# Steps of r, k, w and v laid in planes from the third tile on, and u times r on ScalarE

## The chip, the cores and the metric

The kernel runs on one core of a Trainium2 chip. Its engines are TensorE (matmuls, PE in the profile, with its weight loads as PEld), VectorE (DVE), ScalarE (ACT), GpSimd (POOL) and SyncE (SP, which issues the DMAs). The metric is the device time of one execution in microseconds. On-chip memory (SBUF) has 128 partitions; matmul results land in PSUM banks.

## The reference

Two parts follow each other. The first is a recurrence over 768 steps, for 4 batches and 8 heads of 48 channels:

```
state = 0
for t in range(S):
    cur = einsum('bhd,bhe->bhde', u[None] * k[t], v[t])
    y[t] = einsum('bhd,bhde->bhe', r[t], state + cur)
    state = w[t][:, :, :, None] * state + einsum('bhd,bhe->bhde', k[t], v[t])
```

The second takes y as 3072 rows of 384 numbers and computes `gelu(y @ w_in) @ w_out`, with w_in 384 x 2048 and w_out 2048 x 384. All is float32.

## The kernel before

The 3072 rows are eight tiles of 384 steps, numbered x = 0 to 7; two tiles make one batch. For each tile there is an attention() generator (the recurrence) and an mlp() generator (the two matrix products). PLAN, a string for each tile, says step by step which generator is advanced next: mlp of tile x-1, attention of tile x, the front part of attention of tile x+1 ("f"), the loads ("l") and sums. So the order on every engine is written out beforehand, and each engine works through its own list in that order.

In attention(), partitions hold channels (two heads of 64 rows, 48 of them used) and the free dimension holds steps. Steps are cut in chunks of C = 64. Inside a chunk the recurrence is a triangular 64 x 64 matrix for each head, built in `a_sb` (named `at` in the code, with source steps on partitions and target steps in columns). Tiles 0 and 1 build it by halving (`halves`). From tile 2 on it is built in this way:

- Blocks of FINE = 4 steps: for each distance 0 to 3, the products of r and k (L404 for distance 0, with u; `apart`, L398, for the others) are summed over channels by `transposed_sums` (L391) and placed by small matmuls (L595). `kx` holds the products, one stretch of it for each step inside a block: the writes of L404 and L398 jump from stretch to stretch with every element.
- Blocks of 16 and 64 steps (`quarters`, h = 4 and h = 16): `plain` (L573, ScalarE) and `lay_out` (L578 and L579, VectorE) put scaled copies of r in `kx`; matmuls (L604) multiply them by k; the results are copied to `a_sb` under masks (L637) at h = 4 and by rows (L620) at h = 16. L658, L665 and L669 scale r and k for the next level by running products of w (`tot`, L424).
- The blocks of 4 are copied under `fine_mask` (L687), two copies of 768 columns.

Then VectorE transposes k (L552) and DMAs move its blocks; kv_ps (L749) gives each chunk's share of the state, L764 chains the states; `inside` (L790) multiplies `a_sb` by v into y_ps; `fences` (L802) read one element of each y bank; L832 adds the product of r and the states to the same banks; ScalarE copies y to `xT` (L858, L855), from which the mlp reads (L1011, L1237).

In `halves` tiles ScalarE scales r by u (L414). In tiles 2 to 7 the steps of r, k and w lie in order: r4, k4 and w4 view them as "p (m a) -> p m a" with a = 4, so that `r4[:, :, 3:4]` is every fourth word. L432 (`times`) multiplies such slices in place.

A load of a tile takes r first, then w, then k, in three DMAs each, then v; w and k have one buffer, r has two. A float32 matmul in the program stands as two records in the trace.

Of the kernel before, what the change touches and what calls it, by code (L numbers as in the profile page):

```python
# [21 lines left out]
C = 64  # L22
G = 64
# [41 lines left out]
def kernel(  # L65
# [87 lines left out]
    places = bufs[0][:, 3 * ALL - FINE * 128:].rearrange("p (a r) -> p a r", a=FINE)  # L153

    def load_first():

        t = bufs[0]
        loaded[0] = [None, None]
        size = 3 * NP * T // units_of(0)
        order = [(i, 2) for i in range(units_of(0))] + [(i, part) for i in range(units_of(0)) for part in (0, 1)]  # L160
        for n, (i, part) in enumerate(order):
            s = slice(i * size + part * size // 3, i * size + (part + 1) * size // 3)
            nc.sync.dma_start(out=t[:, s], in_=rkw[0, :, s])
            if n == 0:
                nc.sync.dma_start(out=u_sb, in_=u)
# [113 lines left out]
    nc.gpsimd.iota(t_all, pattern=[[1, C]], base=0, channel_multiplier=0)  # L279
    nc.gpsimd.iota(t_block, pattern=[[1, C // FINE], [0, FINE]], base=0, channel_multiplier=0)  # L280
    for i, h in enumerate(QUARTERS[:1]):
# [10 lines left out]
    def make_fine():  # L292
        nc.vector.tensor_tensor(out=fine_mask, in0=s_qs[FINE], in1=t_block, op=ALU.is_equal)
        nc.vector.tensor_tensor(out=later, in0=t_all, in1=s_qs[1], op=ALU.is_ge)
        nc.vector.tensor_tensor(out=fine_mask, in0=fine_mask, in1=later, op=ALU.bitwise_and)

        nc.gpsimd.memset(places, 0.0)
        for z in range(4):
            o = slice(z * 32, (z + 1) * 32)
            v = places[o]  # L300
            v = bass.AP(tensor=v.tensor, offset=v.offset, ap=[v.ap[0], [128 + 1, FINE], [FINE, 32]])
            nc.gpsimd.tensor_copy(out=v, in_=ident[o, o].unsqueeze(1).to_broadcast([32, FINE, 32]))

    def make_quarter_masks():
        make_fine()
        yield
        for (h, a), m_q in m_qs.items():
            nc.vector.tensor_tensor(out=quarter[h][a], in0=s_qs[h][:, 0:m_q.shape[1]], in1=m_q, op=ALU.is_equal)
            yield
# [56 lines left out]
    def attention(x, unit):  # L366
# [19 lines left out]

        r4, k4, w4 = (z.rearrange("p (m a) -> p m a", a=FINE) for z in (r, k, w))
        n_m = n_u // FINE

        def transposed_sums(o, e, n):  # L390
# [4 lines left out]
        def apart(e, n):  # L395

            o = sum(FINE - i for i in range(1, e)) * n_m
            nc.vector.tensor_mul(kx[:, o:o + n * n_m].rearrange("p (a m) -> p m a", a=n), k4[:, :, 0:n], r4[:, :, e:e + n])  # L398
            return o

        if x >= 2:
            for q in range(qs):
                m_q = slice(q * T // FINE, (q + 1) * T // FINE)
                nc.vector.scalar_tensor_tensor(out=kx[:, 0:n_u].rearrange("p (a m) -> p m a", a=FINE)[:, m_q],  # L404
                                               in0=r4[:, m_q], scalar=u_sb[:, q:q + 1], in1=k4[:, m_q],
                                               op0=ALU.mult, op1=ALU.mult)
            yield
            transposed_sums(0, 0, FINE)
            yield
        else:  # L410

            rus = [kx[:, b * Q * T:(b + 1) * Q * T] for b in parts]
            for q in range(qs):
                nc.scalar.activation(out=rus[q // Q][:, q % Q * T:(q % Q + 1) * T], in_=r[:, q * T:(q + 1) * T], func=AF.Copy,  # L414
                                     scale=u_sb[:, q0 + q:q0 + q + 1])
            rucs = [ru.rearrange("p (i c t) -> p i c t", c=2, t=C) for ru in rus]
# [3 lines left out]
        for h in LEVELS:  # L420
            nb = n_u // (2 * h)
            t2 = tot[h].rearrange("p (n two) -> p n two", two=2)
            tot[2 * h] = tot_sb[:, at_tot:at_tot + nb]
            nc.vector.tensor_mul(tot[2 * h], t2[:, :, 0], t2[:, :, 1])  # L424
            at_tot += nb
            if x >= 2 and h == 2:
                yield
        if x >= 2:
# [18 lines left out]

            w_01 = tot[2].rearrange("p (m two) -> p m two", two=2)[:, :, 0:1]
            times(k4[:, :, 0:3], w4[:, :, 3:4].to_broadcast([128, n_m, 3]))
            yield  # L450
            times(r4[:, :, 3:4], w4[:, :, 2:3])
            times(r4[:, :, 1:2], w4[:, :, 0:1])
            times(r4[:, :, 2:4], w_01.to_broadcast([128, n_m, 2]))
            yield
# [101 lines left out]
        def quarters():  # L556
# [5 lines left out]

            def views(h):
                m = C // 4 // h
                r4 = r.rearrange("p (n m four j) -> p n m four j", m=m, four=4, j=h)
                t4 = tot[h].rearrange("p (n m four) -> p n m four", m=m, four=4)
                ends = (0, 3 * C // 4, 5 * C // 4, 6 * C // 4)
                return m, r4, t4, *(rx[:, :, i:j].rearrange("p n (m x) -> p n m x", m=m) for i, j in zip(ends, ends[1:]))

            def plain(h):  # L570
                m, r4, t4, s0, s1, s2 = views(h)
                for z, f in ((s0[:, :, :, 0:h], 1), (s1[:, :, :, 0:h], 2), (s2, 3)):
                    nc.scalar.copy(out=z, in_=r4[:, :, :, f, :])  # L573

            def lay_out(h):
                m, r4, t4, s0, s1, s2 = views(h)
                z = s1[:, :, :, h:]
                nc.vector.tensor_mul(z, r4[:, :, :, 3, :], t4[:, :, :, 2:3].to_broadcast(z.shape))  # L578
                nc.vector.tensor_mul(s0[:, :, :, h:], s1, t4[:, :, :, 1:2].to_broadcast(s1.shape))  # L579

# [4 lines left out]
            for h in QUARTERS:  # L585
# [36 lines left out]
                def copy_quarters(first, behind, d):  # L622
# [5 lines left out]
                    if m == 1:  # L628
                        copy_rows(first, behind, d, slice(None))
                        return  # L630
                    an = at[:, :, first:behind].rearrange("p g n (m x) -> p g n m x", m=m)
                    o = 0
                    for a in range(3):
                        w_q = (3 - a) * C // 4
                        mask = quarter[h][a].rearrange("p (m x) -> p m x", m=m).unsqueeze(1).unsqueeze(1)
                        data = d[:, :, :, o:o + w_q].rearrange("p g n (m x) -> p g n m x", m=m)
                        nc.vector.copy_predicated(out=an[:, :, :, :, (a + 1) * h:], mask=mask.to_broadcast(data.shape), data=data)  # L637
                        o += w_q
# [17 lines left out]

                z = r4[:, :, :, 1:, :].rearrange("p n m b j -> p n m (b j)")
                nc.vector.tensor_mul(z, s0, t4[:, :, :, 0:1].to_broadcast(z.shape))  # L658
                yield
                if not last:  # L660
                    plain(4 * h)
                k4 = k.rearrange("p (n four j) -> p n four j", four=4, j=h)
                z = k4[:, :, 0:2, :].rearrange("p n b j -> p n (b j)")
                t2 = tot[2 * h].rearrange("p (n two) -> p n two", two=2)
                nc.vector.tensor_mul(z, z, t2[:, :, 1:2].to_broadcast(z.shape))  # L665
                yield
                z = k4.rearrange("p n (b two) j -> p n b two j", two=2)[:, :, :, 0, :]
                tz = t4.rearrange("p n m (b two) -> p (n m) b two", two=2)[:, :, :, 1:2]
                nc.vector.tensor_mul(z, z, tz.to_broadcast(z.shape))  # L669
                yield  # L670
# [11 lines left out]
                if h == FINE:  # L682
                    mask = fine_mask.rearrange("p (m b) -> p m b", b=FINE).unsqueeze(1)
                    for g in range(2):
                        data = fine_of(ds[-1], g).rearrange("p (b n) -> p n b", n=n_b)
                        data = data.unsqueeze(2).to_broadcast([128, n_b, C // FINE, FINE])
                        nc.vector.copy_predicated(out=at[:, g].rearrange("p n (m b) -> p n m b", b=FINE),  # L687
                                                  mask=mask.to_broadcast(data.shape), data=data)
                        yield

# [88 lines left out]
        def inside():  # L779

            for b in range(np_):
# [5 lines left out]
                for i in range(NI):  # L787
                    for p in range(2):
                        for g in range(2):
                            nc.tensor.matmul(y[p][half[g ^ swap(b)], i * C:(i + 1) * C], lhsT=vs(b, i, g)[half[p]],  # L790
                                             rhs=at[half[p], g, b * NI + i, :], start=(i == 0), stop=True, skip_group_check=True)
                ys.append((y, None if split else y_ps))
# [19 lines left out]
        else:  # L812
# [4 lines left out]
            yield  # L817
            inside()
            fences()
            yield  # L820

        for i in range(NI):
            for p in range(2):
                for b in range(np_):
                    q, c3 = divmod(i, N3)
                    for g in range(2):
                        c = 2 * c3 + (p + g) % 2
                        src, c0 = (st, c - 1) if c else (before, NC - 1)
                        if src is None:
                            continue  # L830
                        o = ((parts[b] * Q + q) * NC + c0) * D
                        nc.tensor.matmul(ys[b][0][c % 2][half[g ^ swap(b)], i * C:(i + 1) * C],  # L832
                                         lhsT=src[half[g], o:o + G], rhs=rc[half[g], b, i, c % 2],
                                         start=False, stop=True, skip_group_check=True)
# [642 lines left out]
```

## Time and profile before

| | |
|---|---|
| median of 3 runs | 589.5 us (588.08 to 589.55) |
| profiled execution | 592.28 us, span 590.5 us |
| busy in the span | PE 571.7, DVE 462.9, ACT 275.9, POOL 8.0 us |
| granted TensorE clock | 1.0 |
| L790, a_sb by v | 768 records, 96 a tile |
| L832, r by the states | 704 records, 80 or 96 a tile |

A row of a group reads: line, engine, operation, output and inputs, shapes, count, then total busy us and mean ns of one, then the idle time of the engine before them and what ended it. In the list of waits a row gives who waited, for whom, the total in us, how many times, and the longest. In the row of tenths each digit is the busy share of one fortieth of the span. Matmuls are pipelined: their recorded lengths (218 ns for 64 columns) overlap, so the price of one is taken from the length of a whole group in the chain divided by its records.

### The profile page before, as it was taken

How to read it: one execution, taken by the hardware profiler on the slowest of the kernel's cores; microseconds unless marked ns; L12 is line 12 of the kernel's file. 1: busy time of each engine (PE TensorE's matmuls, PEld its weight loads, DVE VectorE, ACT ScalarE, POOL GpSimd, SP SyncE). 2: the span in 40 equal slices, each digit the busy share in tenths (PEclk: the TensorE clock that was granted, in tenths of full speed). 3: DMA queues.
4: the chain of work that ended last, by engine and by line, in shares of the span. 5: the costliest groups of instructions: out<-in, count | busy, mean ns of one | idle time of the engine just before them, and what ended most of it. 6: DMA issues, size and time to landing. Idle time of an engine off the chain costs nothing. (4 is left out here: it accounts for less than half of the span.)

```text
span 590.5 us, 17425 instructions
## 1 busy us (share of the span) xinstructions
PE 571.7 (97%) x7505; PEld 508.1 (86%) x7517; DVE 462.9 (78%) x907; ACT 275.9 (47%) x640; POOL 8.0 (1%) x21
## 2 busy tenths in 40 slices
PE   7769999999999999999999999999999999999998
PEld 3566666766799999999999999999998999999997
DVE  7879767988968986787859987688758998975532
ACT  2458889323612558046461468145560465523400
POOL 3100000000000000000000000000000000000000
PEclk9999999999999999999999999999999999999999
DMA  7649661120142301341023311330015200210000
GB/s 245 206 138 354 211 232 56 34 88 2 29 139 78 109 3 31 98 125 38 1 42 104 122 38 21 93 115 7 3 31 163 73 2 2 41 39 8 1 14 33
DMA packets 51004, 46.80 MB, mean 79 GB/s; under 512 B 31728, under 2 KB 36080, under 8 KB 50928
## 3 DMA queue, kind: packets, MB, share of 16 engines
q1 hardware_dynamic: 50832, 45.62, 25.4%
q8 instruction: 59, 0.97, 0.7%
q14 instruction: 17, 0.14, 0.1%
q10 hardware_dynamic: 96, 0.07, 0.1%
HBM read 36.24 MB, written 4.72 MB: 69 GB/s over the span
## 5 line engine op out<-in xcount | busy, mean ns | idle before, releaser
L1011 PE MATMUL h_ps<-xT,w_in_sb 128*128 128x192 f32 x408 | 81.2, 330 | 0.7 <-DVE o_sb L1360 0.6
L1011 PEld LDWEIGHTS h_ps<-xT,w_in_sb 128*128 128x128 f32 x408 | 67.8, 190 | 3.7 <-ACT g L1043 1.2
L1223 PE MATMUL h_ps<-xT,w_in_sb 128*128 128x384 f32 x192 | 64.1, 490 | 0.1
L1223 PEld LDWEIGHTS h_ps<-xT,w_in_sb 128*128 128x128 f32 x192 | 35.9, 190 | 23.9
L1237 PE MATMUL o_ps<-w_out_sb,g 128*128 128x192 f32 x224 | 39.5, 326 | 0.0
L1237 PEld LDWEIGHTS o_ps<-w_out_sb,g 128*128 128x128 f32 x224 | 36.9, 190 | 0.3
L620 ACT COPY a_sb<-d 32x256 f32<-32x256 f32 (+8 forms) x90 | 32.6, 362 | 4.6 <-PE d L604 3.1
L1237 PE MATMUL o_ps<-w_out_sb,f 128*128 128x192 f32 x176 | 31.7, 330 | 0.0
L1237 PE MATMUL o_ps<-t,g 128*128 128x192 f32 x176 | 31.4, 329 | 0.0
L1237 PE MATMUL o_ps<-w_out_sb,e 128*128 128x192 f32 x176 | 31.3, 328 | 0.0
L1237 PE MATMUL o_ps<-t,s 128*128 128x192 f32 x176 | 30.9, 327 | 0.0
L1237 PE MATMUL o_ps<-t,e 128*128 128x192 f32 x176 | 30.9, 327 | 0.0
L637 DVE COPY_PREDICATED a_sb<-quarter,d 128x480 f32<-128x480 uint8 (+5 forms) x54 | 23.1, 437 | 8.6 <-PE d L604 7.3
L465 PEld LDWEIGHTS d<-rkw 64*64 64x64 f32 x1152 | 19.1, 134 | 12.2 <-issue 8.5
L764 DVE SCALAR_TENSOR_TENSOR st<-st,tot_sb,kv_ps 128x48 f32<-128x48 f32 x160 | 28.9, 257 | 0.9 <-PE kv_ps L749 0.8
L1011 PE MATMUL u_ps<-s,w_in_sb 128*128 128x192 f32 x160 | 29.5, 327 | 0.0
L1237 PEld LDWEIGHTS o_ps<-t,g 128*128 128x128 f32 x176 | 28.7, 190 | 0.4
L1237 PEld LDWEIGHTS o_ps<-w_out_sb,e 128*128 128x128 f32 x176 | 28.8, 190 | 0.3
L1237 PEld LDWEIGHTS o_ps<-w_out_sb,f 128*128 128x128 f32 x176 | 28.7, 190 | 0.4
L1237 PEld LDWEIGHTS o_ps<-t,s 128*128 128x128 f32 x176 | 28.8, 190 | 0.1
L1237 PEld LDWEIGHTS o_ps<-t,e 128*128 128x128 f32 x176 | 28.8, 190 | 0.1
L604 PE MATMUL d<-kx,rkw 64*64 64x96 f32 x1056 | 28.2, 248 | 0.0
(236 smaller groups left out, 1163.6 us busy)
## 6 DMA issues: line engine op xcount, KB each, us to landing
rkw<-in_rkw_dram SPq DMA_DIRECT2D x54, 256.0 KB, 4.0
raw<-in_w_out_dram SPq DMA_DIRECT2D x8, 768.0 KB, 5.2
v_in<-in_v_dram SPq DMA_DIRECT2D x8, 584.0 KB, 4.1
raw<-in_w_in_dram SPq DMA_DIRECT2D x5, 768.0 KB, 8.8
out_dram<-o_sb SPq DMA_DIRECT2D x20, 192.0 KB, 2.2
rkw<-kx SPq DMA_DIRECT2D x72, 48.0 KB, 2.0
rkw<-in_rkw_dram SPq DMA_DIRECT2D x6, 384.0 KB, 5.7
raw<-in_w_in_dram SPq DMA_DIRECT2D x9, 256.0 KB, 3.3
```

The source lines that it names most:

```text
L465: nc.tensor.matmul(d[half[p], g, n * width:(n + 1) * width], lhsT=kc[half[g], b, i, p], rhs=right(half[g], b, i, p), start=True, stop=True)
L604: nc.tensor.matmul(o[half[p], i * 3 * C // 2:(i + 1) * 3 * C // 2], lhsT=kc[half[g], n // NI, n % NI, p], rhs=rx[half[g], 2 * n + p], star ...
L620: nc.scalar.copy(out=at[z, g, first:behind, (a + 1) * h:], in_=d[z, :, :, to] if g == slice(None) else d[z, :, to])
L637: nc.vector.copy_predicated(out=an[:, :, :, :, (a + 1) * h:], mask=mask.to_broadcast(data.shape), data=data)
L764: nc.vector.scalar_tensor_tensor(out=stq[:, q, c], in0=stq[:, q, c - 1] if c else b4[:, q, NC - 1], scalar=totq[:, q, c:c + 1], in1=kvs[q ...
L1011: nc.tensor.matmul(o, lhsT=lhsT, rhs=rhs, start=start, stop=True, skip_group_check=True)
L1223: nc.tensor.matmul(h_ps, lhsT=w_in_sb[:, f // FI, j, f % FI * 128:(f % FI + 1) * 128], rhs=xT[:, j, :], start=(j == 0), stop=(j == NJ - 1))
L1237: nc.tensor.matmul(o, lhsT=lhs(j), rhs=rhs(j), start=start and j == 0, stop=(j == HF - 1), skip_group_check=True)
```

## The change

For tiles 2 to 7 the host lays each group of 16 steps in planes: the first steps of its four blocks of 4, then the four second steps, and so on. v is permuted in the same way on its partitions. So the words of r, k and w that belong to one step inside a block lie in runs of four. The code follows: r4, k4, w4 become "p (b a m) -> p b a m", `apart` and the product with u write `kx` in its own order, the h = 4 level runs over blocks in the innermost dimension, masks and `places` are made for the new order, and the fine copy becomes four instructions of 384 columns for both heads instead of two of 768.

Two things move between engines or are added: r is scaled by u on ScalarE (four instructions of 384 elements a tile) and VectorE multiplies the result by k in one instruction of 1536; GpSimd clears `a_sb` once more after tile 1's `inside`, since what lies above the diagonal is laid out anew.

The rows of y must come out in the order of the steps. The matmuls of L790 and L832 read their moving operand through `in_order`, which walks b, then m, then a: from column to column 4 words, or 16 bytes.

```
+    def planes(x):
+        return x >= 2
+    def in_order(x, z):
+        return z.rearrange("p (b a m) -> p b m a", a=FINE, m=FINE) if planes(x) else z
...
-    nc.gpsimd.iota(t_block, pattern=[[1, C // FINE], [0, FINE]], base=0, channel_multiplier=0)
+    nc.gpsimd.iota(t_block, pattern=[[FINE, C // 16], [0, FINE], [1, FINE]], base=0, channel_multiplier=0)
...
     def make_fine():
-        nc.vector.tensor_tensor(out=fine_mask, in0=s_qs[FINE], in1=t_block, op=ALU.is_equal)
+        nc.vector.tensor_scalar(out=s_block, in0=s_qs[1], scalar1=4, scalar2=2,
+                                op0=ALU.logical_shift_right, op1=ALU.logical_shift_left)
+        nc.vector.tensor_scalar(out=s_low, in0=s_qs[1], scalar1=FINE - 1, scalar2=None, op0=ALU.bitwise_and)
+        nc.vector.tensor_tensor(out=s_block, in0=s_block, in1=s_low, op=ALU.bitwise_or)
+        nc.vector.tensor_tensor(out=fine_mask, in0=s_block, in1=t_block, op=ALU.is_equal)
...
-        r4, k4, w4 = (z.rearrange("p (m a) -> p m a", a=FINE) for z in (r, k, w))
+        r4, k4, w4 = (z.rearrange("p (b a m) -> p b a m", a=FINE, m=FINE) for z in (r, k, w))
+        def by_planes(z):
+            return z.rearrange("p (a b m) -> p a b m", b=n_16, m=FINE)
+        def of_planes(z, i, j):
+            return z[:, :, i:j, :].rearrange("p b a m -> p a b m")
...
-            nc.vector.tensor_mul(kx[:, o:o + n * n_m].rearrange("p (a m) -> p m a", a=n), k4[:, :, 0:n], r4[:, :, e:e + n])
+            nc.vector.tensor_mul(by_planes(kx[:, o:o + n * n_m]), of_planes(k4, 0, n), of_planes(r4, e, e + n))
...
-                nc.vector.scalar_tensor_tensor(out=kx[:, 0:n_u].rearrange("p (a m) -> p m a", a=FINE)[:, m_q],
-                                               in0=r4[:, m_q], scalar=u_sb[:, q:q + 1], in1=k4[:, m_q],
-                                               op0=ALU.mult, op1=ALU.mult)
+                nc.scalar.activation(out=by_planes(kx[:, 0:n_u])[:, :, b_q], in_=of_planes(r4, 0, FINE)[:, :, b_q], func=AF.Copy,
+                                     scale=u_sb[:, q:q + 1])
+            z = by_planes(kx[:, 0:n_u])
+            nc.vector.tensor_mul(z, z, of_planes(k4, 0, FINE))
...
             def plain(h):
+                    if h == FINE:
+                        nc.scalar.copy(out=z[..., 0], in_=r4[..., f])
...
             def lay_out(h):
+                if h == FINE:
+                    z, last = s1[..., 1], r4[..., 3]
+                    rest = s0[..., 1:]
...
-                        nc.vector.copy_predicated(out=an[:, :, :, :, (a + 1) * h:], mask=mask.to_broadcast(data.shape), data=data)
+                        nc.vector.copy_predicated(out=an[:, :, :, :, a + 1:], mask=mask.to_broadcast(data.shape), data=data)
...
-                    for g in range(2):
-                        nc.vector.copy_predicated(out=at[:, g].rearrange("p n (m b) -> p n m b", b=FINE),
-                                                  mask=mask.to_broadcast(data.shape), data=data)
+                    for a in range(FINE):
+                        z, f, m_a = rows[:, :, :, a], fine[:, :, a], mask[:, a]
+                        nc.vector.copy_predicated(out=z, mask=m_a, data=f)
...
-                                             rhs=at[half[p], g, b * NI + i, :], start=(i == 0), stop=True, skip_group_check=True)
+                                             rhs=in_order(x, at[half[p], g, b * NI + i, :]), start=(i == 0), stop=True, skip_group_check=True)
...
+            if planes(x + 1) and not planes(x):
+                nc.gpsimd.memset(a_sb, 0.0)
...
-                                         lhsT=src[half[g], o:o + G], rhs=rc[half[g], b, i, c % 2],
+                                         lhsT=src[half[g], o:o + G], rhs=in_order(x, rc[half[g], b, i, c % 2]),
...
+    z = rkw[2:].reshape(-1, T // 16, FINE, FINE)
+    rkw[2:] = z.swapaxes(-1, -2).reshape(rkw[2:].shape)
+    z = v[2:].reshape(-1, 8, FINE, FINE, v.shape[2])
+    v[2:] = z.swapaxes(2, 3).reshape(v[2:].shape)
```

## The prediction

> **What bounds the kernel now.** I read the page's first two parts, then the chain that ended last, then PE's own list of waits without the start, and last the groups by shape for the operations that the change touches. In the chain, a row is start, length, engine, tile, line and number of records.
>
> ```profile
> PE 571.7 (97%) x7505; PEld 508.1 (86%) x7517; DVE 462.9 (78%) x907; ACT 275.9 (47%) x640; POOL 8.0 (1%) x21
> PE   7769999999999999999999999999999999999998
> DVE  7879767988968986787859987688758998975532
> ```
> ```profile
> 492.54 1.97 PE d L604 x80
> ...
> 502.55 10.40 PE o_ps L1237 x64
> ...
> 519.89 1.56 PE y_ps L790 x96
> ...
> 522.95 1.56 PE y_ps L832 x96
> ```
> ```profile
> PE y_ps L832 <- DVE fence L802: 1.3, 1, 1.3
> PE h_ps L1011 <- DVE o_sb L1360: 0.6, 1, 0.6
> PE kv_ps L749 <- DMA rkw<-kx: 0.5, 1, 0.5
> PE y_ps L790 <- DVE st L764: 0.3, 1, 0.3
> PE h_ps L1011 <- DVE o_sb L1334: 0.2, 1, 0.2
> ```
>
> TensorE is a wall from the fourth slice on. The last list is PE's whole idle time from 130 us to the end: 2.9 us. So a faster VectorE can give back at most 2.9 us, while every nanosecond that a matmul gains in length between 130 us and the end is paid in full. The chain also gives prices: 192 columns on the whole array take 10.40 / 64 = 162.5 ns a record, 0.85 ns a column. Matmuls on a quarter of the array (64 rows by 64 columns) run four at a time: 96 columns cost 1.97 / 80 = 24.6 ns a record, 64 columns 1.56 / 96 = 16.25 ns.
>
> The groups by shape show what a stride costs:
>
> ```profile
> L424 DVE TENSOR_TENSOR tot_sb<-rkw 128x768 f32<-128x768 f32 x7 | 6.5, 934 | 0.0
> L398 DVE TENSOR_TENSOR kx<-rkw 128x1152 f32<-128x1152 f32 x3 | 6.6, 2204 | 0.0
> L398 DVE TENSOR_TENSOR kx<-rkw 128x384 f32<-128x384 f32 x3 | 2.6, 865 | 0.1
> L432 DVE TENSOR_TENSOR rkw<-rkw 128x384 f32<-128x384 f32 x12 | 10.2, 871 | 0.2
> L432 DVE TENSOR_TENSOR rkw<-rkw 128x1152 f32<-128x1152 f32 x6 | 8.1, 1346 | 0.0
> L578 DVE TENSOR_TENSOR kx<-rkw,tot_sb 128x384 f32<-128x384 f32 x12 | 6.6, 552 | 0.1
> ```
>
> L578 moves 384 elements in runs of four: 552 ns. L398 with 384 elements reads every fourth word of r and of k and writes contiguously: 865 ns (860 over both kinds of tile). L424 reads every second word and pays nothing (934 ns for 768; L665 of that size takes 958). So on VectorE reading in steps of 16 bytes costs (860 - 552) / 384 = 0.80 ns an element, and steps of 8 bytes nothing. L398 with 1152 elements, whose output jumps 1536 bytes from element to element, pays (2204 - 1346) / 1152 = 0.74 ns.
>
> **The change, part by part.** PE, SP and DMA issue the same instructions in the same order as before; the loads have the same bytes, laid out on the host. All that changes is access patterns, four added ScalarE instructions a tile, VectorE's groups, and a little of POOL.
>
> *Matmuls (the term that decides).* The moving operands of L790 (a_sb) and L832 (r) now go through in_order: the four steps of a block lie 16 bytes apart, so each matmul reads 64 columns in steps of 16 bytes. L790 has 768 records in eight tiles, 96 a tile; L832 has 704, 80 in the first tile of a batch and 96 in the second. From the third tile on (three batches): 6 x 96 + 3 x 176 = 1104 records, now 1104 x 16.25 ns = 17.9 us. No row shows TensorE reading in steps of 16 bytes, so the price has bounds. Low end: nothing, if its reads have room. Far end: VectorE's rows give 1.06 ns an element without a penalty (552 and 958 ns for 384 and 768) over a base of 146 ns, hence (860 - 146) / 384 = 1.86 ns an element with one; two quarters read from the same 64 partitions, and if they took turns at 1.86 ns, four records would need 64 x 1.86 x 2 = 238 ns, 59.5 each: 43.3 ns more, 47.8 us. I take the only read penalty that the trace has, 0.80 ns an element: 64 x 0.80 = 51 ns per matmul in its quarter, four at once, 12.8 ns a record: 1104 x 12.8 ns = 14.1 us. With 1.86 ns as the whole price of a column it is 119 / 4 = 29.8 ns a record, 14.9 us; with the 12 ns that a 64-column matmul now has beyond its columns (65 - 64 x 0.83) added back, 18 us. If those 12 ns are slack instead, the excess is (51 - 12) / 4 = 9.8 ns a record, 10.8 us. None of it is hidden: both groups lie in the chain.
>
> [...]
>
> *VectorE, each tile.* Gone: four L404 of 883 ns (3.53 us), L398 of 2.20 + 1.54 + 0.86 us, three L432 of 0.87. In their place: one multiply of 1536 elements at 1.76 (L518's row of that size), L398's successors at full speed (1.35 + 0.95 + 0.55, by L432's and L578's rows), three of 0.55. Saved: 1.77 + 1.75 + 0.96 = 4.5 us. Added: L578 now reads r in 16-byte steps (+0.31); copies under the masks write runs of 3, 2 and 1 words, of which the last has 16-byte steps (160, 160 and 64 elements by 0.80: +0.31); the fine copy becomes four of 384 instead of two of 768 (L637 by size: 1.11 ns an element and 158 fixed: 2.33 for 2.03, +0.30). Net 3.6 us a tile, 21 us in all, VectorE to about 441 us. Nearly all of it lies beside PE.
>
> What reaches PE: around 455 us the fence waited behind L404, which started when its load landed (453.93 to 456.9). With ScalarE's part done before, VectorE needs 1.76 instead of 3.01 us there, 1.25 us sooner, and PE's wait of 1.27 us for L802 goes; what is late next is nothing, PE continues. The wait of 0.56 us for L1360 at 466 us sits behind the same backlog and L398: it goes too. The other three stay: the one for the DMA moves, 0.5, follows transposes whose input waits for PE at 295 us, and that for L764 follows kv_ps. Together -1.8 us; ends 0 and -2.9.
>
> *ScalarE, each tile.* Four scalings of r by u: 4 x 605 ns (L414's row, same shape) = 2.4 us, in the gap where it now sits idle before ysb L858: 6.7 to 7.4 us in the four tiles I looked at. They need only r, loaded ahead of w and k; if r were late, L858 and the copies to xT would queue behind them and the next x sums with them, but that gap is 4 us longer than they are. The plain copies of the finer level read 16-byte steps: 3 x 384 elements at 0 to 0.80 ns, up to +0.9 us; VectorE's multiply behind them comes 3 us sooner than now, so PE does not see it. Cost 0.
>
> *POOL and start.* The added memset of a_sb costs 1.4 us (L267's row), after tile 1's last L790 (106 us); the next write to a_sb is at 136.7 us, 30 us of cover. Three added mask operations of 0.19 us (L258's row) run on VectorE in tile 1's stage, beside L1223. Cost 0.
>
> *Sum.* 14.1 - 1.8 = +12.3 us. The profiled execution took 592.28 us (span 590.5 and 1.8 around it), 2.8 above the median of 589.5; 604.6 for a like execution, 601.8 against the median.
>
> **The rivals.**
> 1. *TensorE reads such steps at full rate.* For it: a column lasts 0.85 ns here and the quarters have spare time (64 columns take 65 ns, and 48 columns in L749 take 64), so a slower fetch could partly vanish. Against it: the slack is some 12 ns, the expected excess 51. Then only the waits go: 589.5 - 1.8 = 587.7, at best 586.6. This ends on the other side; it decides as soon as the penalty per column is under about (12 + 6.5) / 64 = 0.3 ns, where slack and the 1.8 us together cover it. [...]
> 2. *A part is hidden in that slack*: 3 to 8 us gross (3 to 7 ns a record), 591 to 596.
> 3. *Quarters take turns at the same partitions*: up to +47.8 - 2.9, about 634. Against it: 64-column quarters today need 16.25 ns a record, so their reads do overlap.
> 4. *ScalarE's new work delays an eviction.* It would need to hold a PSUM bank that PE wants; PE's list shows no wait for ScalarE, PEld's some 1.7 us. Inside the ranges.
>
> **How the numbers follow.** Forecast (10.8 to 18 us gross; less the waits of 1.8 to 2.9: 597.5 to 606.5) 0.52; rival 1 0.34; rival 2 0.08; rival 3 0.06. Predicted: 601.8. The range, 587.0 to 606.5, holds the forecast's case, rival 2 and most of rival 1; the forecast's own range is 597.5 to 606.5. Faster by over 0.3% (about what a measurement of this kernel can tell, 1.8 us) is the better half of rival 1: 0.20; within 0.3%: 0.13; slower: 0.67.
>
> **What would show it.** Right: L790 and L832 of late tiles at some 29 ns a record, 2.8 us for 96, while those of the first two tiles keep 16; PE's waits after 130 us near 1 us; L398's successors at 1.35, 0.95 and 0.55 us; VectorE near 441 us, ScalarE near 291 or above. Wrong: L790 and L832 at 16 ns, when the end moves by the waits alone.

## The result: 4.4% slower, twice the loss that was forecast

| | us | ratio to before, 95% interval |
|---|---|---|
| before, median of 4 | 589.01 | |
| after, median of 4 (612.33 to 617.16) | 614.61 | 1.0437, 1.0393 to 1.0481 |
| forecast | 601.8 (587.0 to 606.5) | |
| profiled execution, before and after | 592.28 and 614.64 (spans 590.5 and 612.9) | |

The sign was right. The loss of 25.6 us is twice the 12.3 of the forecast and lies outside its range. The page of the kernel after, first the busy times and then the row of tenths of PE:

```profile
PE 587.7 (96%) x7505; PEld 523.2 (85%) x7517; DVE 458.6 (75%) x904; ACT 294.5 (48%) x664; POOL 8.2 (1%) x22
PE   6789999999999989999999999999999999999998
```

PE works 16 us longer with the same 7505 records. The chain of the kernel after shows where (start, length, engine, tile, line, records; L841 is L790 of before, L885 is L832):

```profile
103.82 1.71 PE y_ps L841 x96
...
147.96 1.99 DVE a_sb L738 x4
...
173.72 2.97 PE y_ps L841 x96
...
224.44 1.89 DVE a_sb L738 x4
...
578.73 31.21 PE o_ps L1290 x192
```

The group of tile 1, still in the old layout, takes 1.71 us. The group of tile 2 takes 2.97 us, 30.9 ns a record instead of 16.25. Over 1104 records that is 1104 x 14.65 ns = 16.2 us. And VectorE's masked copies stand in the chain: L738 is the fine copy under the mask. (The chain of before can be followed back only to 465 us, so it does not say whether they stood in it earlier; the waits do.) PE's list of waits after 130 us (who, for whom, us in total, times, longest) says what that costs:

```profile
PE d L646 <- DVE a_sb L738: 5.4, 4, 1.4
PE d L637 <- DVE a_sb L679: 3.6, 4, 1.1
PE kv_ps L800 <- DMA rkw<-kx: 0.4, 1, 0.4
PE y_ps L841 <- DVE st L815: 0.3, 1, 0.3
```

L646 and L637 are the matmuls into `d` (L604 and L595 before; L637 of the kernel before is another line, the masked copy that is L679 now). They come in bursts, each of which fills one pair of PSUM banks. Before, PE waited 2.9 us in this stretch and never for these. Now it waits 9.7 us, 9.0 of them for a masked copy to release a pair. The forecast's two waits, for L1360 and for the fence L802, are gone from the stretch.

The profile adds up: 16.2 of longer matmuls, 9.0 of new waits, 2.2 of old waits gone: 23.0, against 22.4 between the two spans. (The median has grown by 3 us more because the profiled execution of before was 3.3 us above its median.)

The groups by shape, first of before, then of after, show which operations came out as worked out and which did not:

```profile
L637 DVE COPY_PREDICATED a_sb<-quarter,d 128x480 f32<-128x480 uint8 x12 | 8.3, 689 | 7.3 <-PE d L604 7.3
L637 DVE COPY_PREDICATED a_sb<-quarter,d 128x320 f32<-128x320 uint8 x12 | 6.0, 501 | 0.4
L637 DVE COPY_PREDICATED a_sb<-quarter,d 128x160 f32<-128x160 uint8 x12 | 4.0, 335 | 0.4
```
```profile
L621 DVE TENSOR_TENSOR kx<-kx,tot_sb 128x768 f32<-128x768 f32 x12 | 11.5, 958 | 9.2 <-ACT kx L608 8.6
L427 DVE TENSOR_TENSOR kx<-kx,rkw 128x1536 f32<-128x1536 f32 x6 | 10.5, 1758 | 7.5 <-ACT kx L424 5.7 <-DMA rkw<-in_rkw_dram 1.8
L679 DVE COPY_PREDICATED a_sb<-quarter,d 128x320 f32<-128x320 uint8 x12 | 10.5, 874 | 0.4
L679 DVE COPY_PREDICATED a_sb<-quarter,d 128x160 f32<-128x160 uint8 x12 | 10.5, 872 | 0.4
L679 DVE COPY_PREDICATED a_sb<-quarter,d 128x480 f32<-128x480 uint8 x12 | 10.4, 870 | 3.3 <-PE d L646 3.3
L457 DVE TENSOR_TENSOR rkw<-rkw 128x384 f32<-128x384 f32 x12 | 6.4, 554 | 0.2
L418 DVE TENSOR_TENSOR kx<-rkw 128x1152 f32<-128x1152 f32 x3 | 4.0, 1350 | 0.0
```

L418, L457 and L427 take what was expected (1.35, 0.55 and 1.76 us). L679 is the surprise: the three copies of a group take 0.87 us each, whether 480, 320 or 160 elements. Before they took 0.69, 0.50 and 0.34. All of L679 together takes 38.5 us instead of 23.1.

### The profile page after: what moved, and what is told of

Same layout as the page of the kernel before. It is cut to its first block, busy times and chain, and to the rows that moved or that the text cites. A ratio compares the mean times of both kernels' runs of the same rounds, so it can differ in the third digit from the quotient of the medians.

```text
span 612.9 us, 17445 instructions
## 1 busy us (share of the span) xinstructions
PE 587.7 (96%) x7505; PEld 523.2 (85%) x7517; DVE 458.6 (75%) x904; ACT 294.5 (48%) x664; POOL 8.2 (1%) x22
## 3 DMA queue, kind: packets, MB, share of 16 engines
q1 hardware_dynamic: 50832, 45.62, 24.8%
## 4 chain that ended last, share of the span: by engine, by line
PE 85%; DVE 9%; issue 2%; DMA 2%; SPq 2%; ACT 0%; DVEq 0%
PE o_ps L1290 31%; PE h_ps L1064 13%; PE u_ps L1064 10%; PE h_ps L1276 9%; DVE a_sb L679 5%; PE d L490 4%; PE y_ps L841 4%; PE o_ps L1370 3%; PE y_ps L885 3%; PE d L646 3%; PE kv_ps L800 2%; PE c_ps L1064 2%; DVE a_sb L738 1%; SPq L572 1%; DMA rkw<-in_rkw_dram 1%
## 5 line engine op out<-in xcount | busy, mean ns | idle before, releaser
L679 DVE COPY_PREDICATED a_sb<-quarter,d 128x480 f32<-128x480 uint8 (+5 forms) x54 | 38.5, 748 | 4.5 <-PE d L646 3.3
L646 PE MATMUL d<-kx,rkw 64*64 64x96 f32 x1056 | 28.7, 248 | 5.4 <-DVE a_sb L738 5.4
L646 PEld LDWEIGHTS d<-kx,rkw 64*64 64x64 f32 x1056 | 23.3, 133 | 11.6 <-DVE a_sb L738 4.7
L1290 PE MATMUL o_ps<-t,s 128*128 128x192 f32 x176 | 30.9, 327 | 0.0
L1290 PE MATMUL o_ps<-t,e 128*128 128x192 f32 x176 | 30.9, 327 | 0.0
L911 ACT COPY ysb<-y_ps 128x384 f32<-128x384 f32 x8 | 3.8, 478 | 53.2 <-PE y_ps L885 46.2
```

The source lines that it names most:

```text
L646: nc.tensor.matmul(o[half[p], i * 3 * C // 2:(i + 1) * 3 * C // 2], lhsT=kc[half[g], n // NI, n % NI, p], rhs=rx[half[g], 2 * n + p], star ...
L679: nc.vector.copy_predicated(out=an[:, :, :, :, a + 1:], mask=mask.to_broadcast(data.shape), data=data)
L1290: nc.tensor.matmul(o, lhsT=lhs(j), rhs=rhs(j), start=start and j == 0, stop=(j == HF - 1), skip_group_check=True)
```

## Do the two costs stand alone? Four kernels

Theory A: two independent costs, 16 us of strided reads on TensorE and 9 us of PE waits that the slow masked copies make. Rival B: the waits are a consequence of the longer matmuls. Rival C: the waits come from ScalarE's plain copies (L608, L573 before, takes 0.90 instead of 0.51 us, and VectorE's L621 waits 8.6 us for them). Each kernel takes one cost out of the kernel after or puts one into the kernel before.

**Contiguous columns in the kernel after.**

```
     def in_order(x, z):
-        return z.rearrange("p (b a m) -> p b m a", a=FINE, m=FINE) if planes(x) else z
+        return z
```

> The kernel after, but L790's and L832's successors (L841, L885) read their 64 columns contiguously; the rows of y come out in the order of the planes, so the reordering is left out. Theory A (16 us from the strided reads, added to 9 us of new PE waits that come from slow masked copies): both lines back to about 16.3 ns a record, the 9 us of waits stay, time about 598 us (+9 on before). Rival B (the waits are a consequence of the longer matmuls, which shift the engines against each other): waits go too, 587 to 590 us.

Measured: 598.35 us, ratio to before 1.0145 (1.0123 to 1.0168). The chain of this kernel has its late groups back at 16.25 ns, and its waits are those of the kernel after:

```profile
174.09 1.56 PE y_ps L841 x96
```
```profile
PE d L646 <- DVE a_sb L738: 5.4, 4, 1.4
PE d L637 <- DVE a_sb L679: 3.6, 4, 1.1
```

So the waits do not hang on the longer matmuls: rival B falls.

**Strided columns in the kernel before.**

```
+    def in_order(x, z):
+        return z.rearrange("p (b a m) -> p b m a", a=FINE, m=FINE) if x >= 2 else z
...
-    rhs=at[half[p], g, b * NI + i, :]
+    rhs=in_order(x, at[half[p], g, b * NI + i, :])
...
-    rhs=rc[half[g], b, i, c % 2]
+    rhs=in_order(x, rc[half[g], b, i, c % 2])
```

> The kernel before with one part of the change: from the third tile on, L790 and L832 read their columns in steps of 16 bytes (the rows of y are then in a wrong order). Theory A: about 31 ns a record instead of 16.3, +16 us, less up to 1.8 us of waits that the longer matmuls cover: 603 to 605 us, no new PE waits. Rival B: new PE waits of several us appear here as well, 610 us or more.

Measured: 604.14 us, ratio 1.0248 (1.0225 to 1.0272), +15.3 us. The chain and the whole list of PE's waits after 130 us (L793 is L790):

```profile
171.98 2.97 PE y_ps L793 x96
```
```profile
PE y_ps L793 <- DVE st L767: 0.7, 2, 0.4
```

The late groups take 30.9 ns a record as in the kernel after, 16.2 us in all, and the longer matmuls cover some 2 us of the old waits (0.7 us are left of 2.9). No new wait comes with them.

**Long runs in the masked copies of the kernel after.**

```
-    an = at[:, :, first:behind].rearrange("p g n (m x) -> p g n m x", x=4)
+    an = at[:, :, first:behind].rearrange("p g n (m x) -> p g n m x", m=m)
...
-    nc.vector.copy_predicated(out=an[:, :, :, :, a + 1:], mask=...
+    nc.vector.copy_predicated(out=an[:, :, :, :, (a + 1) * h:], mask=...
```

(mask and data are cut into the same runs.)

> The kernel after, but the masked copies at h = 4 (L679) write and read runs of 12, 8 and 4 words as before the change instead of 3, 2 and 1 (the same numbers of elements, to wrong columns). Theory A: L679 falls from 38.5 to about 23 us, PE's waits on L738 and L679 from 9 us to under 2, time about 605 us. Rival C (the waits come from ScalarE's plain copies, 0.90 instead of 0.51 us each, which hold up the layout of r): the waits stay at 6 us or more, 611 us or more.

Measured: 605.38 us, ratio 1.0266 (1.0233 to 1.0299), 9.2 us less than the kernel after. All of PE's waits after 130 us:

```profile
PE y_ps L841 <- DVE st L815: 0.7, 2, 0.4
```

ScalarE's plain copies are as slow in this kernel as in the kernel after, VectorE still waits 8.7 us for them, and PE's list has no wait that follows from it. Rival C falls.

```profile
L608 ACT COPY kx<-rkw 128x384 f32<-128x384 f32 x18 | 15.1, 908 | 0.0
```

**Short runs in the masked copies of the kernel before** (the same edit the other way round, three words in a run of the first copy, two and one in the others).

> The kernel before with one part of the change: masked copies at h = 4 (L637) in runs of 3, 2 and 1 words (to wrong columns). Theory A: each of the three in a group takes 0.87 us whatever its number of elements, L637 from 23 to about 38 us, and PE waits 5 to 9 us for it and the fine copies: 594 to 598 us. Rival C: VectorE has the room, 589 to 591 us.

Measured: 598.33 us, ratio 1.0156 (1.0141 to 1.0171), +9.5 us. The smallest of the three copies (the other two take 0.87 us as well), and the two longest of PE's waits in this kernel:

```profile
L637 DVE COPY_PREDICATED a_sb<-quarter,d 128x160 f32<-128x160 uint8 x12 | 10.5, 872 | 0.4
```
```profile
PE d L604 <- DVE a_sb L687: 5.1, 4, 1.3
PE d L595 <- DVE a_sb L637: 3.6, 4, 1.1
```

The two costs, each put alone into the kernel before, give 15.3 + 9.5 = 24.8 us. The whole change costs 25.6. Within what the intervals allow, that is the loss.

## What is left of the change without them

> The kernel after without both costs: contiguous columns for L841 and L885, and masked copies in runs of 12, 8 and 4 words (the reordering of y is left out, and the masked copies go to wrong columns). Theory A (these two are the whole loss, the rest of the change is the forecast's saving): 586.7 to 588.5 us, PE's waits after 130 us at most 1.3 us. Rival D (a third cost: ScalarE's slower plain copies, the memset, a different start): 589.5 us or more.

Both edits on the kernel after. Measured over 12 runs: 588.29 us, ratio 0.9998 (0.9976 to 1.0020). There is no third cost that can be measured, but no gain either, and the forecast's 1.8 us is not there. PE's waits come to 2.1 us, where at most 1.3 were expected. The waits after 130 us in this kernel, and the part of VectorE's timeline ahead of the first of them (start, length, instruction, and in brackets the idle time before it):

```profile
PE y_ps L885 <- DVE fence L853: 1.1, 1, 1.1
PE kv_ps L800 <- DMA rkw<-kx: 0.7, 1, 0.7
PE y_ps L841 <- DVE st L815: 0.3, 1, 0.3
```
```profile
453.44 1.76 DVE L427 TENSOR_TENSOR kx<-kx,rkw 128x1536 f32<-128x1536 f32 x1 [2.71 <-DMA rkw<-in_rkw_dram]
455.11 0.35 DVE L1398 TENSOR_TENSOR u<-o_ps,rkw 128x192 f32<-128x192 f32 x1
455.38 0.21 DVE L853 COPY fence<-y_ps 128x2 f32<-128x2 f32 x2
```

The multiply is 1.25 us shorter, as worked out, and the fence still comes 1.1 us late, because the multiply waits for a load (here from 450.7 to 453.4 us). PE reaches this point 1.47 us earlier than before (L841 at 451.38 instead of 452.85), the multiply starts only 0.49 us earlier (453.44 instead of 453.93). The load has taken the place of the long instruction as what ends this wait. VectorE's saving lies ahead of the first burst of matmuls into `d`, where it had time to spare: before, it stood idle for 7.3 us in all until those bursts had ended (the row of L637 with 480 elements).

**u times r on ScalarE alone, in the old layout.**

```
-                nc.vector.scalar_tensor_tensor(out=kx[...a planes...], in0=r4[:, m_q], scalar=u_sb[:, q:q + 1], in1=k4[:, m_q], ...)
+                nc.scalar.activation(out=kx[:, q * T:(q + 1) * T], in_=r[:, q * T:(q + 1) * T], func=AF.Copy, scale=u_sb[:, q:q + 1])
+            nc.vector.tensor_mul(kx[:, 0:n_u], kx[:, 0:n_u], k)
...
-            transposed_sums(0, 0, FINE)
+            nc.vector.tensor_reduce(..., in_=kx[:, 0:n_u].rearrange("p (n j a) -> p a n j", j=32, a=FINE), ...)
```

> The kernel before with u times r alone moved to ScalarE: r keeps its layout, ScalarE writes u times r in the order of the steps, VectorE multiplies by k in place (1536 contiguous), and the sum over channels reads every fourth word. Nothing is left out. The multiply takes 1.76 instead of 3.5 us, the sum about 3.0 instead of 1.77 us. PE's wait of 1.3 us for the fence goes, that for L1360 stays: 587.2 to 588.0 us if the waits of the profile are worth their length; 589 if another wait takes their place.

Measured over 9 runs: 591.09 us, ratio 1.0058 (1.0038 to 1.0079): slower, where 587.2 to 589 was expected. The multiply takes 1.76 us and the sum 2.98, as expected, and the wait for the fence is gone. In its place PE waits at the start of the next tile's products:

```profile
PE h_ps L1012 <- DVE o_sb L1361: 1.3, 2, 0.7
PE h_ps L1012 <- DVE u L1354: 0.7, 1, 0.7
PE h_ps L1012 <- DVE o_sb L1335: 0.4, 1, 0.4
```

That is 2.4 us where before had 0.8. The sum, 1.2 us longer, runs on VectorE directly behind the fence (454.29 to 457.2 us) and ahead of the instructions that PE waits for at 463 to 465 us; that it makes these waits is read from this order and was not tested by itself. In the profile the waits after 130 us come to 2.9 us, as before, so why the median is some 3 us higher stays open.

## What a strided column costs TensorE

Three kernels change only the pattern in which L790 and L832 of the kernel before read their 64 columns from the third tile on; one reads strided columns with the whole array.

```
pairs:    z.rearrange("p (n two w) -> p two n w", two=2, w=2)
step 8:   z.rearrange("p (n two) -> p two n", two=2)
step 32:  z.rearrange("p (n eight) -> p eight n", eight=8)
whole:    L1223: rhs=xT[:, j, :].rearrange("p (b a m) -> p b m a", a=FINE, m=FINE)
```

> The kernel before, with the columns of L790 and L832 from the third tile on read in pairs of neighbouring words, pair after pair 16 bytes apart (wrong order of rows). If what costs is a new 16-byte line for every column, a line is now used twice in a row: about 62 to 70 ns for 64 columns a quarter, 16.3 to 18 ns a record, 589 to 591 us. If every jump costs: 20 ns or more a record, 595 us or more.

> The same matmuls read every second word (steps of 8 bytes; wrong order of rows). As VectorE pays nothing for such steps: 16.3 ns a record, 588 to 590 us. If any step beyond one word costs: 20 ns or more a record, 595 us or more.

> The same matmuls read every eighth word (steps of 32 bytes; wrong order of rows). If the price is one new line a column: as with 16 bytes, about 31 ns a record, 604 us. If it grows with the step: more than 33 ns, 607 us or more.

> The kernel before, but the 192 records of 384 columns on the whole array in L1223 (first two tiles' products) read their columns in steps of 16 bytes (the columns are then in a wrong order). Now 331 ns a record. If each column in such steps takes about 1.74 ns whoever reads, as the quarter matmuls of L841 came to (123.6 ns for 64 columns, less 12): 384 x 1.74 = 668 ns a record, +65 us, 650 us or more. If only two quarters that read the same partitions get in each other's way: no change, 589 us.

| columns | us | ratio, 95% interval | price |
|---|---|---|---|
| pairs of words, 16 bytes apart | 588.93 | 1.0000 (0.9972 to 1.0028) | 16.4 ns a record |
| every second word (8 bytes) | 589.43 | 1.0035 (1.0003 to 1.0068) | 16.4 ns a record |
| every fourth word (16 bytes) | 604.14 | 1.0248 (1.0225 to 1.0272) | 30.9 ns a record |
| every eighth word (32 bytes) | 605.97 | 1.0298 (1.0268 to 1.0328) | 31.0 ns a record |
| every fourth word, whole array, 384 columns | 655.54 | 1.1154 (1.1117 to 1.1191) | 682 to 687 ns a record instead of 331 |

The row of every fourth word is the kernel with strided columns above. The last two kernels ran twice each. The last price is (655.54 - 588.11) / 192 = 351 ns a record on top of the 331 of before; the trace has 24 such records from 191.01 us to the next group at 207.51, 687 ns each. That line of PE's timeline, and then the chains of two of the other kernels, first pairs, then steps of 32 bytes (a group of L793 is again 96 records):

```profile
191.01 16.57 PE L1223 MATMUL h_ps<-xT,w_in_sb 128*128 128x384 f32 x24
```
```profile
516.62 1.57 PE y_ps L793 x93
```
```profile
172.28 2.98 PE y_ps L793 x94
...
321.38 2.98 PE y_ps L793 x96
```

(Three records of the group of pairs are missing from the trace, and two of the first group of 32 bytes.) Two columns in a row from the same 16 bytes cost nothing that these runs can tell, in pairs or in steps of 8 bytes (16.4 ns a record, against 16.25 for contiguous columns). One column from each 16 bytes costs 682 / 384 = 1.78 ns with the whole array (1.79 by the trace). For a quarter, four records at 30.9 are 123.6 ns for 64 columns; contiguous ones take 65 ns, 10.6 more than 64 columns at 0.85 would. If those 10.6 ns stay as they are, a strided column costs (123.6 - 10.6) / 64 = 1.77 ns. So the two quarters that read the same partitions do not get in each other's way, and a step of 32 bytes costs a record no more than one of 16 (31.0 and 30.9 ns). The 8-byte kernel's ratio lies 0.35% above 1, yet neither its matmuls nor its waits are longer; where that comes from is not shown.

## What a short run costs a masked copy

> The kernel before with masked copies (L637) in runs of 6, 4 and 2 words (to wrong columns), 80 runs each in the first two groups. If a run costs at least four words of time (4.45 ns): 0.69, 0.50 and 0.50 us. If a run is rounded up to a multiple of four words: 0.87, 0.50 and 0.50 us. If every run costs a fixed addition beside its words: 0.69 plus more for the first, and the third below the second. Time 590 to 594 us.

The edit is that of the short runs, with 6, 4 and 2 words. Measured: 589.90 us, ratio 1.0027 (1.0009 to 1.0045).

```profile
L637 DVE COPY_PREDICATED a_sb<-quarter,d 128x480 f32<-128x480 uint8 x12 | 10.4, 868 | 7.3 <-PE d L604 7.3
...
L637 DVE COPY_PREDICATED a_sb<-quarter,d 128x320 f32<-128x320 uint8 x12 | 6.0, 500 | 0.4
L637 DVE COPY_PREDICATED a_sb<-quarter,d 128x160 f32<-128x160 uint8 x12 | 6.0, 498 | 0.4
```

Runs of 2 cost as much as runs of 4. The rows of before give 158 ns and 1.11 ns a word; with each run counted up to a multiple of four words, 80 runs of 6 are 640 words, 158 + 640 x 1.11 = 0.87 us, as measured (a mere minimum of four words a run would have left 0.69). The 160 runs of the kernel after are 640 words too, which is why its three copies took the same time. PE's waits for masked copies come to 1.8 us in this kernel, between the none of before and the 8.7 with the shortest runs.

One row stands out: 192 elements in 64 runs of 3 take 624 ns in the kernel after, where 256 words would be 0.44 us. This copy comes directly behind the one in 160 runs of one word, and it is not alone in that place. L700, an ordinary multiply (L658 before), is slower in half of its executions, 1.56 us instead of 1.35, and these are the ones directly behind such a copy. Its own pattern is not the reason: the first row is the kernel after with long runs in the masked copies, the second the kernel before with short ones.

```profile
L700 DVE TENSOR_TENSOR rkw<-kx,tot_sb 128x1152 f32<-128x1152 f32 x12 | 16.2, 1350 | 0.0
```
```profile
L658 DVE TENSOR_TENSOR rkw<-kx,tot_sb 128x1152 f32<-128x1152 f32 x12 | 17.5, 1458 | 0.0
```

So the instruction behind a masked copy in 160 runs of one word took some 0.2 us longer. Why is not shown.

## The main cost mended

TensorE reads contiguous columns, and ScalarE puts y in order as it copies it from PSUM to `xT`:

```
+   for c in range(2):
+       copy(out=o[:, c].rearrange("p i (b m a) -> p i b m a", a=FINE, m=FINE),
+            in_=y[s][:, c].rearrange("p i (b a m) -> p i b m a", a=FINE, m=FINE))
...
```

> The kernel after with its main cost mended: TensorE reads contiguous columns, and ScalarE puts the rows of y in order when it copies them from PSUM (L911, L908): 14 copies a tile of 192 elements that read PSUM in steps of 16 bytes, instead of 7 of 384. Nothing is left out. Theory A: 16 us less than the kernel after, 598 us as with contiguous columns alone, if ScalarE's copies end before the products of the next tile need them; at 0.52 us each (192 elements from PSUM at 0.32, and 0.2 more for the steps) they take 3.9 us a tile more, and the gap before the sums of xT is about 3 us, so up to 1 us a tile of new PE waits: 598 to 604 us. Rival: the steps cost as much there as on TensorE, 610 us or more.

Measured: 600.01 us, ratio 1.0193 (1.0147 to 1.0239), 14.6 us better than the kernel after. ScalarE's copies take the time of contiguous ones (L1279 of before: 319 ns for 192 elements):

```profile
L911 ACT COPY xT<-y_ps 48x192 f32<-48x192 f32 x72 | 19.0, 313 | 0.4
```

PE's waits are the 9.0 us for the masked copies and 1.0 of others. ScalarE is busy 2.4 us longer in all (296.9 for 294.5). So the reordering has a place where it costs nothing that these runs can tell: the interval overlaps with that of the contiguous columns alone (1.0123 to 1.0168). The masked copies remain. No version that was run beats the kernel before.

## Why the forecast was wrong, point by point

- **The matmuls (14.1 us): right in kind, too small by 2.** Measured 16.2. The excess per column is 0.92 ns (14.65 x 4 / 64), not the 0.80 of VectorE's rows, and none of it vanished in slack. It lay inside the term's own range of 10.8 to 18. That a price taken from another engine came so near is in part luck: no row tied the two together.
- **The step that failed: "of which the last has 16-byte steps ... +0.31", and "Nearly all of it lies beside PE".** The masked copies were priced by the step between words, 0.31 us a tile. Measured was a count by runs, each up to a multiple of four words (0.87 us for 480, 320 and 160 elements alike, in 160 runs): 15.4 us in all, 2.6 a tile. And they were set against what VectorE saves elsewhere. The saving (L427, L418, L457) lies ahead of the first burst of a tile; the masked copies lie between two bursts and hold the PSUM pairs that the next burst needs. VectorE is less busy than before (458.6 us for 462.9), and PE waits 9.0 us for it all the same. This term was missing from the sum and from the range. The rest of VectorE's account was right: with long runs and contiguous columns it is busy 443.2 us, where about 441 was forecast.
- **The waits (-1.8 us): the number came about, for another reason.** In the kernel after, 2.2 us of old waits are gone, but the kernel with strided columns and nothing else loses as much: the longer matmuls cover them. A faster VectorE alone does not: in the kernel without the two costs the fence waits 1.1 us behind a load. "What is late next is nothing" was wrong; it was a load into `rkw`.
- **ScalarE: no cost to PE, as said.** The scalings took 0.60 us each and fit the gap. The plain copies cost more than the bound (0.39 us more each, for 0.31), and VectorE waited 8.6 us for them; with long runs PE did not notice.
- **The memset and the new mask operations** left no wait of PE after them.
- **Rivals.** Full rate on TensorE (0.34), a part hidden in slack (0.08, 3 to 7 ns a record where 14.65 were measured) and quarters taking turns (0.06) are out, the last by the whole-array price (1.78 ns a column, and 1.77 in a quarter). The fourth, ScalarE delaying an eviction, has no wait in PE's list. No rival had VectorE's copies as a wait of TensorE, though the list of tiles that both engines touch would have named the pairs `d`.
- **Two figures in the working.** A contiguous 64-column matmul has 10.6 ns beyond its columns, not 12, when the column is the 0.85 ns of the forecast's own row; 0.83 is what the median recorded lengths of 384 and 192 columns give, (486 - 326) / 192 ns (L1223 and L1237 of before). And the upper end of the forecast's own range, 606.5, is 0.8 above what its terms give (589.5 + 18 - 1.8 = 605.7). Neither changes the outcome.

## What to carry to other kernels

An engine's saving and its losses may not be added up over a tile: ask of each instruction which buffer it holds and who wants that buffer next. When a layout is changed so that one engine reads in runs, write down the pattern that every other engine then reads and writes, and price each by the words it takes from each 16 bytes. With one word, TensorE took 2.1 times as long here (682 ns for 331, whole array), a copy on ScalarE 1.8 times (0.90 us for 0.51, L608 and L573) and a multiply on VectorE 1.6 times (0.87 us for 0.55, L432 and L457); with two words, TensorE and VectorE lost nothing (16.4 ns a record for 16.25; 934 ns for 768 elements, L424, where L665 takes 958), and ScalarE was not measured. A masked copy went by its runs here (0.87 us for 160 runs of 1, 2 or 3 words) and needs a price of its own. A reordering that has to stay somewhere cost nothing measurable where ScalarE reads PSUM anyway (313 ns for 192 elements, 319 in a row).

## What was not expected of the hardware

- TensorE took 1.77 to 1.79 ns for a float32 column that is alone in its 16 bytes, instead of 0.85, whether a quarter or the whole array read; in quarters, steps of 16 and 32 bytes cost the same (30.9 and 31.0 ns a record). With two columns from the same 16 bytes in a row, it paid nothing that could be told (16.4 ns a record, against 16.25).
- A masked copy counted each run up to a multiple of four words (0.87 us for 160 runs of 1, 2 or 3 words and for 80 runs of 6), and the instruction directly behind 160 runs of one word took some 0.2 us longer; an ordinary multiply of 1152 elements in runs of 3 (L700) paid nothing for its own pattern (1.35 us).
- ScalarE paid 1.02 ns an element (0.39 us for 384: 0.90 in L608, 0.51 in L573) for reading SBUF in steps of 16 bytes and nothing for reading PSUM in such steps (313 ns for 192 elements, 319 in a row).
